# A new sequence of turns for a kernel of linear attention and an MLP, with the last chunk's buffers claimed by whoever comes first

## The chip, the core and the metric

The kernel runs on one core of one Trainium2 chip. A core has five engines that each work through their own instructions in order and wait for one another by semaphores: TensorE (PE, with its weight loads shown apart as PEld), VectorE (DVE), ScalarE (ACT), GpSimd (POOL) and SyncE (SP, which here only issues DMAs). The metric is the time of one execution on the device in microseconds (us); less is better. A line such as L857 is line 857 of the kernel's file.

## What is computed

A gated linear attention over B=4 batches, H=8 heads, S=768 steps and D=48 elements a head, then a layer norm and a two-layer network with ReLU and a residual, all in fp32:

```python
for t in range(S):
    state = alpha[:, :, t, :, None] * state + np.einsum('bhd,bhe->bhde', k[:, :, t], v[:, :, t])
    y[:, :, t] = np.einsum('bhd,bhde->bhe', q[:, :, t], state)
x = y.transpose(0, 2, 1, 3).reshape(B, S, H * D)          # 4 x 768 x 384
xn = (x - mu) / np.sqrt(var + 1e-06) * g_ln
out = x + np.maximum(xn @ w_ch1, 0.0) @ w_ch2             # 384 -> 1536 -> 384
```

The weights come in as float64.

## The kernel before

*Chunks and turns.* The 768 steps are cut into six chunks of 128. Each pair of chunk and batch has one Python generator of attention work, 24 in all; in the order string they are the letters a to x (a to d are chunk 0's batches, e to h chunk 1's, and so on). Each generator yields after every small step. Other letters stand for the network and the weights. The string ORDER (L33 to L53) has 1508 letters; the loop at L938 calls `next` on the generator of each letter, one after the other, under a manual schedule. So the string fixes the order in which instructions are issued on every engine at once: each engine works through its instructions in the order in which the turns emitted them. Nothing reorders them later. Buffers are handed out by pools with fixed counts; one that is reused makes its next writer wait for its last reader. One such pool holds six banks of PSUM (tag "bank", L353, L384, L452, L680, L851 and others) that all kinds of products share.

*An attention turn by turn.* Load q, k, v and alpha (`load`, L123 to L168); logarithm (L312) and running sums by a small matmul; exponentials on ACT (L324, L325); k and q scaled on DVE (L327, L329, "qk"); one gate row to DRAM and back; transposes to kT and qT, in chunks 0 and 1 by PE (L355, copied out at L360 and L362), later by DVE and DMA; the scores (L397 or L405, with the running sums of a later generator between them at L407); a masked copy into "at" (L415, L420); the state's update (L432 on PE, L445 on DVE, L447 on POOL). Then the **y product** (L463 and L467): 32 small matmuls into two banks, one with kT's state and one with the scores. ACT copies the first bank out (L493; L483 and L484 in the last two chunks) and DVE adds the second to it. Layer norm and a transpose give xT (L530 and L532 by PE in chunks 0 to 3). POOL zeroes "at" again at L499 for the last two batches of chunk 0.

*Weights.* Twelve pieces A to L are loaded as 64-bit words and turned into fp32 with integer operations on DVE (L219 to L236) and one on ACT (L227).

*The network.* For chunk 0 it is done directly: Y and Z are the two halves of the hidden layer (L567, three matmuls of 256 columns each), P and Q the second layer (L579 with an add at L583). For chunks 1 to 5 it runs by a bilinear algorithm that spends additions on fewer products. Turns "1" and "2" are the two row halves of the first layer: 15 **hidden products** for each chunk (`hidden_product`, L857, two matmuls of 256 columns), whose sums go to the hidden buffers with copies on ACT and adds on DVE and POOL (L864 to L900) and ReLUs on ACT (turns R and U, L907). Turn "M" is the second layer: 20 **products** for each chunk (`product`, L683), each four matmuls of 192 columns in one turn and in the next turn their adds into the output (L693 for an addition on DVE, L696 for a subtraction, L730 and others copies on ACT, L699 late adds on POOL, and a send to DRAM, L558). Operands of the products are sums of blocks: turn W combines the second weights (L643), S the first (L809), X the inputs of a chunk's hidden products (`combine_x`, L834, eleven turns a chunk), N the hidden blocks (`combine_hidden`, L670, sixteen turns a chunk, into buffers called sum0 to sum5 and in place). Turn O loads a kept x for the residual (L554).

*The last chunk's buffers.* Chunk 5's hidden buffers are not taken from the pools: `buffers_of_last` (L601) puts them together out of attention buffers that are no longer used (at, qk, eq), one more xT and three input buffers, once, at its first call; its callers are `third_of` (L595) and `combine_x` (L818). A hidden product of the last chunk takes its u buffers from `late_of["u"]` before it comes to `third_of`, so it needs the claim to have been made: in this order, the first last-chunk X turn is turn 1279, ahead of the first hidden product of that chunk.

Of the kernel before, what the change touches and what calls it, by code (L numbers as in the profile page):

```python
# [30 lines left out]


ORDER = (  # L33
    "bacabcadaacbcaadbcadabcababbebaccbadbaaBbccaedcbceAeeaaacbfecfBcdafddeaedbdeafae"
    "bcdccbfgadhAdcgCcdbebeebfhggdfgbfffbCdcgfgecdfchgdfhgabcddchdhAiiegjhacehedhhjfg"
    "biAdfidAeBhBijffYYiCjZZYYifZYlZCgjYDlYYjjZZYBZYgDieEgDgDjZZekEhZYGZgZigZGeeYgYgg"
    "fZYEhfGfkChihiYFYijfgEhgkhFZYhgYfghijgkFeZZlGZShfZYHlhHfYFYZeZHelYiZgllPmZkJIgJk"
    "PeiYjJIflHeSZIQgkIlYSjiPkffennSQlOKjLSnSjmSQhKnSjLnKPkiljnhSQnLkkjkWknkShOmPhkhl"
    "kOOhWlmmphmQmkmXjWQnXjlSQjPmkilXSXkP2OXWjXQjkjW2iXoSWX2oWX22Pi2mnol1j1mom2omSpoo"
    "l1XSpk2oW2m112p1m2pm11m1W211pp12O122r22jnn21lpnmnjSml1riOn2l12Rl111kqS1m21W1Rkp2"  # L40
    "o21mUXpq1mU2rUrnmj1rl2Rno2oomqonrormpokO1rNM2Mipin1op1ionoqUM2qp2W12RkMmNqiMoRtk"
    "UrpkqNM1NoMliMlNUMMNMNMKNqMlNorMWrnmtltNRMsqppMWNMriMMMpNlsqqqnoqttNttMtMsXMMssM"
    "sMNMNMX1oXXppMvstM2MXMMNMsppXoMXoqMsMMXM1nqqv11Xq1trMq2tqX21rn12v1r2ur2r222rvsqs"
    "svsu1rs1nuvvt2s11ss11p22rtsvosn2uropuXru222221uts212stnU1211u1121222Op1Rp2tRU21R"
    "Us1pXqU11x2tO2MM1vwMUM12xuRvu1vurNNNNwtOuuMwRxvNtxRNutwwMM2MOwNXwMNuXMMtNM1rMMMw"
    "qtXMMMxNUNxtMMsNMMMxXxMtXtrMMqMNrMXNvutMMwNuMMMNMMMxMLMOM11vvuq2X2O2wMus1wX11222"
    "2r2Xt1222w22utsqxvw2x2ww1vx21sX12121xwvq2O2x2w111u1uvU121w12s1wuRvx12U11J1q21R1U"
    "OvRxU121wMMu2xxsRNMw2NNMRM1MUNN2MMuUMqXN1MrNNRMNvMXNXMMMM2MMMxNM1uNXMMNMNMOXMXMv"
    "MMXOMMMXxNxwxMMvNMMMMMXMx21w1x222212v12w222x122w2212X11UX2212121121121wx111MU11X"
    "2RR2v1211212211R1URU211XOUM2XNRX1MX1RM2MXN2MXNXNMXXMXMMMN111U1MN1M1122MNM1MM2MM1"  # L50
    "11NNN121O11NM1MM21N1112N1122M1MMM12MM12N222M22M2RM1M2N22MM2MU1ON2M22M2UURR22RNNM"
    "MNM1MMOMRMNMUUM2ONMNNNMO2MMMUMNMMMMMRMMNNMMMNMNMMNMMMMMMMMNMNMMMMMMM"
)  # L53


# [1 line left out]
def kernel(  # L57
# [42 lines left out]
    NCB = S // P  # L100
# [491 lines left out]
    def third_of(c, t, h):  # L592

        if c + 1 == NCB:
            buffers_of_last()  # L595
            return late_of["h"][t * 2 + h]
        if c not in hT_of:
            hT_of[c] = work.tile([P, NJ, B, P], FP32, name="hT", tag="hT", bufs=1)
        return hT_of[c][:, t * NT:(t + 1) * NT, h * HB:(h + 1) * HB]

    def buffers_of_last():  # L601
        if "h" in late_of:
            return
        more_x = work.tile([P, NF, B, P], FP32, name="xT", tag="xT").rearrange("p f b t -> p (f b t)")
        free = [raw.tile([P, 2, 2, NP, D], FP32, name=f"r{n}", tag="in", bufs=7).rearrange(
            "t b i p d -> t (b i p d)") for n in "akq"]
        h = [t.rearrange("k p i s t -> k (p i s t)") for t in ats]
        h += [t.rearrange("t n p i c -> t (n p i c)") for t in qks[:3]]
        h.append(more_x[:, :NT * HB * P])
        late_of["h"] = [t.rearrange("p (j b t) -> p j b t", b=HB, t=P) for t in h]  # L610
        sums = [t.rearrange("t p i c -> t (p i c)") for t in eqs[:2]]
        sums += [more_x[:, NT * HB * P:]] + [t[:, 512:] for t in free]
        late_of["x"] = [t[:, i * HB * P:(i + 1) * HB * P]
                        for t in sums for i in range(t.shape[1] // (HB * P))]
        late_of["u"] = [t[:, :512] for t in free]
# [154 lines left out]
    def first_weights_ready():  # L770
        if "a" not in first_of:
            first_of["a"] = {n: [w1[:, 2 * t:2 * t + 2, f]]
                             for n, t, f in ((7, 2, 1), (10, 1, 0), (13, 0, 1), (8, 0, 0))}
        return first_of["a"]
# [5 lines left out]
    def x_ready(c):  # L780
        if ("b", c) not in first_of:
            b = x_blocks(c)
            first_of["b", c] = {0: b[3], 4: b[2], 6: b[0], 11: b[5], 12: b[1]}
        return first_of["b", c]
# [56 lines left out]

    def hidden_product(c, r, n):

        if n == FIRST[0]:
            for i in range(3):
                u = late_of["u"][i] if c + 1 == NCB else work.tile(
                    [P, 512], FP32, name="u", tag="sum", bufs=11)
                first_of["u", c, r, i] = u.rearrange("p (j t) -> p j t", j=2)
        cs = [third_of(c, t, h)[:, 2 * r:2 * r + 2].rearrange("p j b t -> p j (b t)")
              for t in range(3) for h in range(2)]  # L850
        acc = ps.tile([P, 2, HB * P], FP32, name="hps", tag="bank", bufs=6)  # L851
        a, b = first_weights_ready()[n], x_ready(c)[n]
        for i in range(2):
            j = 2 * r + i
            w = a[j // 2][:, 0] if len(a) == 2 else a[0][:, j // 2]
            w = w[:, j % 2 * P:][:, :P]
            nc.tensor.matmul(acc[:, i], w, b, start=True, stop=True)  # L857
        yield
        u0, u1, u2 = (first_of["u", c, r, i] for i in range(3))
        c0, c1, c2, c3, c4, c5 = cs  # L860
        add, sub = nc.vector.tensor_add, nc.vector.tensor_sub
        add_late, sub_late = nc.gpsimd.tensor_add, nc.gpsimd.tensor_sub

        if n == 3:  # L864
            nc.scalar.copy(out=c5, in_=acc)
        elif n == 7:
            add(c4, acc, c5)
        elif n == 5:
            add(c2, acc, c4)
        elif n == 1:  # L870
            add(u0, acc, c2)
        elif n == 10:
            nc.scalar.copy(out=u1, in_=acc)
        elif n == 9:
            sub(u2, u1, acc)
            add_late(c4, c4, u2)
        elif n == 4:
            sub(c2, c2, acc)
            add_late(c2, c2, u1)  # L879
        elif n == 14:  # L880
            add(u2, acc, u2)
            add_late(c0, u0, u2)
            add_late(c0, c0, c1)
        elif n == 6:
            add(c4, acc, c4)
        elif n == 11:
            nc.scalar.copy(out=c1, in_=acc)
        elif n == 2:
            add(c0, acc, c0)
        elif n == 13:  # L890
            sub(c3, u0, acc)
            add_late(c1, c1, c3)
        elif n == 8:
            sub(u2, u2, acc)
            add_late(c1, c1, u2)
            add_late(c5, c5, u2)
        elif n == 0:
            sub(c3, c3, acc)
        else:
            sub(c5, c5, acc)  # L900
        yield
# [8 lines left out]
    def hidden_products(r):  # L910
        for c in range(1, NCB):
            for n in FIRST:
                yield from hidden_product(c, r, n)
# [55 lines left out]
```

## Time and profile before

Three runs took 420.14, 420.69 and 421.5 us (median 420.69). The profiled execution took 420.64 us, of which 418.9 us is the span that the profile shows.

| what | us | share of the span | instructions |
|---|---|---|---|
| time of the profiled execution | 420.64 | | |
| its span | 418.9 | | 11553 |
| PE busy | 409.0 | 98% | 4608 |
| PE's weight loads busy | 360.9 | 86% | 4608 |
| DVE busy | 351.4 | 84% | 713 |
| ACT busy | 178.0 | 42% | 440 |
| POOL busy | 153.2 | 37% | 169 |

| line and work on PE | busy us | instructions |
|---|---|---|
| L857, hidden products with combined inputs | 46.3 of matmul | 192 |
| L857, hidden products with xT itself | 34.0 | 136 |
| L683, products (w, hT), (ws, sum), (ws, hT) | 40.5, 28.7, 23.6 | 224, 160, 128 |
| L579, second layer of chunk 0 | 33.0 | 96 |
| L567, first layer of chunk 0 | 32.5 | 144 |
| L463 and L467, y products | 22.0 and 22.7 | 320 each |

How to read it: the matmuls of PE overlap one another and their weight loads, so a line's busy sum is longer than the time that it adds to the span. A PE that is busy 98% of the time is in effect one long queue of matmuls; what a step costs there is read from the start of one instruction to the start of the next. The clock that was granted to TensorE is 1.00 in every stretch. HBM moves 140 GB/s as a mean over the span, most of it in the first half.

### The profile page before, as it was taken

The numbers are of one execution on the slowest core, as the hardware profiler recorded it, in microseconds if no ns is written. First come the engines' busy times: TensorE is split into PE (matmuls) and PEld (weight loads), VectorE is DVE, ScalarE is ACT, GpSimd is POOL, SyncE is SP. The second block draws the span as 40 slices with busy tenths as digits, with TensorE's granted clock in tenths as the row PEclk, the third lists the DMA queues.
The fourth block names the chain that finished last, engine by engine and source line by source line (L and its number), as shares of the span: only waits on it lengthen the run. The fifth ranks groups of instructions, "written<-read, shape, count | busy, mean of one in ns | idle before, by whom it ended". The sixth has DMA issues, their size and how long they took to land.

```text
span 418.9 us, 11553 instructions
## 1 busy us (share of the span) xinstructions
PE 409.0 (98%) x4608; PEld 360.9 (86%) x4608; DVE 351.4 (84%) x713; ACT 178.0 (42%) x440; POOL 153.2 (37%) x169
## 2 busy tenths in 40 slices
PE   6998999999999999999999999999999999999996
PEld 4787888766678889998889999889998899999996
DVE  3999999999999989996888996688876767977873
ACT  5498456724243496414546612364313242014110
POOL 3011000003203990043395033493152940499123
PEclk9999999999999999999999999999999999999999
DMA  7998889987778778587784546433035200001201
GB/s 247 325 297 246 206 201 293 287 194 181 145 221 176 200 167 185 128 195 178 146 215 70 130 105 166 88 95 77 0 114 104 67 1 2 0 20 38 94 20 56
DMA packets 133741, 59.52 MB, mean 142 GB/s; under 512 B 90764, under 2 KB 129804, under 8 KB 133688
## 3 DMA queue, kind: packets, MB, share of 16 engines
q1 hardware_dynamic: 133688, 58.79, 55.1%
q8 instruction: 36, 0.59, 0.6%
q14 instruction: 17, 0.14, 0.1%
HBM read 42.17 MB, written 16.61 MB: 140 GB/s over the span
## 4 chain that ended last, share of the span: by engine, by line
PE 89%; DVE 4%; ACT 2%; DMA 2%; issue 1%; SPq 1%; POOL 0%; POOLq 0%; DVEq 0%
PE hps L857 31%; PE ops L683 30%; PE ops L579 8%; PE hps L567 8%; PE aps L405 3%; PE yps L463 3%; PE yps L467 2%; PE sums L432 2%; DMA rq<-in_q_dram 2%; PE xps L530 1%; PE tps L355 1%; PE aps L397 1%; PE lps L407 1%; SPq L132 1%; DVE w L221 0%
## 5 line engine op out<-in xcount | busy, mean ns | idle before, releaser
L699 POOL TENSOR_TENSOR ob<-ob,u 128x192 f32<-128x192 f32 x40 | 26.3, 668 | 64.5 <-DVE ob L696 48.3
L857 PE MATMUL hps<-sum,w 128*128 128x256 f32 x192 | 46.3, 381 | 0.0
L907 ACT ACTIVATE hT<-hT 128x512 f32<-128x512 f32 x48 | 28.8, 624 | 34.9 <-POOL hT L879 18.5
L447 POOL TENSOR_TENSOR mid<-mid,gate 112x192 f32<-112x192 f32 x20 | 11.4, 568 | 80.0 <-DVE mid L445 33.3
L683 PE MATMUL ops<-w,hT 128*128 128x192 f32 x224 | 40.5, 327 | 0.0
L857 PEld LDWEIGHTS hps<-sum,w 128*128 128x128 f32 x192 | 36.1, 190 | 5.0
L683 PEld LDWEIGHTS ops<-w,hT 128*128 128x128 f32 x224 | 37.1, 190 | 0.7 <-issue 0.2
L857 PE MATMUL hps<-xT,w 128*128 128x256 f32 x136 | 34.0, 380 | 0.0
L579 PE MATMUL ops<-w,hT 128*128 128x384 f32 x96 | 33.0, 491 | 0.0
L567 PE MATMUL hps<-xT,w 128*128 128x256 f32 x144 | 32.5, 382 | 0.0
L567 PEld LDWEIGHTS hps<-xT,w 128*128 128x128 f32 x144 | 27.0, 190 | 4.2
L683 PE MATMUL ops<-ws,sum 128*128 128x192 f32 x160 | 28.7, 327 | 0.0
L857 PEld LDWEIGHTS hps<-xT,w 128*128 128x128 f32 x136 | 25.5, 190 | 3.1
L683 PEld LDWEIGHTS ops<-ws,sum 128*128 128x128 f32 x160 | 26.5, 190 | 0.3
L579 PEld LDWEIGHTS ops<-w,hT 128*128 128x128 f32 x96 | 17.6, 190 | 10.7 <-DVE w L236 0.3
L693 DVE TENSOR_TENSOR ob<-ops,ob 128x192 f32<-128x192 f32 x50 | 17.3, 353 | 10.6 <-PE ops L683 6.5
L447 POOL TENSOR_TENSOR st<-st,gate 112x192 f32<-112x192 f32 x16 | 11.7, 729 | 37.3 <-DVE st L445 25.9
L683 PE MATMUL ops<-ws,hT 128*128 128x192 f32 x128 | 23.6, 328 | 0.0
L463 PEld LDWEIGHTS yps<-st,qT 48*64 48x64 f32 x320 | 19.9, 134 | 4.0 <-issue 2.0
L467 PE MATMUL yps<-vx,at 64*64 64x48 f32 x320 | 22.7, 219 | 0.0
L463 PE MATMUL yps<-st,qT 48*64 48x48 f32 x320 | 22.0, 220 | 0.6 <-ACT x L493 0.6
L405 PEld LDWEIGHTS aps<-qT,kT 48*64 48x64 f32 x576 | 19.0, 134 | 4.1 <-issue 0.8
(255 smaller groups left out, 1134.2 us busy)
## 6 DMA issues: line engine op xcount, KB each, us to landing
ws<-in_moe_w_ch_dram SPq DMA_DIRECT2D x12, 768.0 KB, 5.9
td<-tr SPq DMA_DIRECT2D x64, 96.0 KB, 3.1
vn<-in_v_dram SPq DMA_DIRECT2D x12, 384.0 KB, 4.3
kept<-x SPq DMA_DIRECT2D x20, 192.0 KB, 3.0
ob<-kept SPq DMA_DIRECT2D x20, 192.0 KB, 3.1
out_dram<-ob SPq DMA_DIRECT2D x19, 192.0 KB, 1.9
ra<-in_alpha_dram SPq DMA_DIRECT2D x16, 192.0 KB, 2.6
kT<-td SPq DMA_DIRECT2D x32, 96.0 KB, 4.2
```

The costliest lines, as they stand in the source:

```text
L405: nc.tensor.matmul(to, kT[rs, p, s], qT[rs, p, s], start=True, stop=True)
L432: nc.tensor.matmul(up[h, p], qk_of(c, b)[ts, 1, p, i, :h.stop - h.start], vn[ts, i, p], start=True, stop=True)
L447: nc.gpsimd.tensor_mul(new, new, by)
L463: nc.tensor.matmul(yps[i][halves[s], i, p], qT[rs, p, s], (now, mid)[s][rs, p], start=True, stop=r != i)
L467: nc.tensor.matmul(yps[r][halves[s], i, p], at[halves[r], p, s], by, start=r != i, stop=True)
L567: nc.tensor.matmul(hps, w1[:, j // 2, f, j % 2 * P:][:, :P], xT_of[0][:, f, bs], start=(f == 0), stop=(f == NF - 1))
L579: nc.tensor.matmul(ops_of[b], hT_of[c][:, j, b], w2[:, j], start=(j == 0), stop=(j == NJ - 1))
L683: nc.tensor.matmul(acc, lhs[:, j], rhs[:, j], start=(j == 0), stop=(j == NT - 1))
L693: nc.vector.tensor_add(x, acc, x)
L699: getattr(nc.gpsimd, f"tensor_{op}")(x, x, y)
L857: nc.tensor.matmul(acc[:, i], w, b, start=True, stop=True)
L907: nc.scalar.activation(out=x, in_=x, func=AFT.Relu)
```

## The change

The change has two parts. Every letter occurs in the new ORDER as often as in the old one, so that each engine issues the same instructions, by line and by shape, with the same buffers and the same DMAs; only their sequence differs, nearly everywhere. And `hidden_product` calls `buffers_of_last` ahead of its u buffers if it belongs to the last chunk: in the new order turn 1303, a "2", is the first to touch that chunk's buffers, and its first X turn is 1306. In the new order lines behind L843 are two lines further down; line numbers in this text are those of before.

```diff
 ORDER = (
-    "bacabcadaacbcaadbcadabcababbebaccbadbaaBbccaedcbceAeeaaacbfecfBcdafddeaedbdeafae"
-    "bcdccbfgadhAdcgCcdbebeebfhggdfgbfffbCdcgfgecdfchgdfhgabcddchdhAiiegjhacehedhhjfg"
+    "aObcacabcaacaddbcaaaababbacdbbbacbccaeababdbcBcecedeaAeOfaacfbcebafcfddefBaeaddd"
+    "AeeccacbdccdbgdCcbbhgedeeccdhffagffgfcdfegCbagdddfghbdcfgbdahggbhiAeijbcehdehhhg"
...
-    "2RR2v1211212211R1URU211XOUM2XNRX1MX1RM2MXN2MXNXNMXXMXMMMN111U1MN1M1122MNM1MM2MM1"
-    "11NNN121O11NM1MM21N1112N1122M1MMM12MM12N222M22M2RM1M2N22MM2MU1ON2M22M2UURR22RNNM"
-    "MNM1MMOMRMNMUUM2ONMNNNMO2MMMUMNMMMMMRMMNNMMMNMNMMNMMMMMMMMNMNMMMMMMM"
+    "21v22RURx21u11221M22N1M2URXXMXXMXMXXR2NXUNM11RXNMN11MMM212212N11N12U1O11MMMMNXM1"
+    "MM1MMN11N12111M2NRX1NMM1M2M121111MNM2M22MM2212N22N22NM2O2M1M2MUMMU2ROMMM1UMRMJO2"
+    "NM2MM2RMN2N2RNMUUNMNO1MMNMNNMMMUMMRMMMMNNMMNMMMMNMMMNMMNMMMNMMMMMMMM"
 )
...
     def hidden_product(c, r, n):
 
+        if c + 1 == NCB:
+            buffers_of_last()
         if n == FIRST[0]:
             for i in range(3):
                 u = late_of["u"][i] if c + 1 == NCB else work.tile(
```

What moves where the prediction looks: three pairs of y products (chunk 2's batches 0, 2, 1 and then chunk 2's batch 3 with chunk 3's batch 0) become neighbours in PE's sequence; chunk 0's transposes, its L312 (ACT), L327 (DVE), L360 (DVE) and the first weight loads change places in the first 40 us; eight of the last chunk's X turns come ahead of the N turn that makes sum5 of chunk 4; and the first of the last two N turns comes ahead of the copy L741.

## The prediction

> **What bounds the kernel now.** I read the page's busy times first, then busy times in five stretches, then the chain of waits where PE pauses, then DVE's timeline at the end.
>
> The stretches (start:end in us, length, then busy us and count for PE, PE's weight loads, DVE, ACT, POOL, and the granted clock):
>
> ```profile
> 8.70:39.60 30.90, 28.43 (x552) 23.34 (x550) 29.57 (x57) 23.67 (x64) 3.09 (x4) 1.00 1.02 306
> 39.70:113.80 74.10, 74.10 (x902) 55.98 (x900) 72.47 (x129) 36.58 (x87) 10.54 (x13) 1.00 0.84 213
> 113.80:116.80 3.00, 2.38 (x130) 2.15 (x129) 3.00 (x7) 1.29 (x4) 0.00 (x0) 1.00 0.63 188
> 116.80:410.00 293.20, 293.10 (x2975) 269.71 (x2976) 240.98 (x502) 111.70 (x277) 133.35 (x136) 1.00 0.44 106
> 410.00:418.90 8.90, 5.68 (x35) 5.38 (x34) 2.99 (x7) 0.32 (x1) 2.87 (x5) 1.00 0.19 66
> ```
>
> The reader is to see that PE is idle for 2.5 us in the first of these stretches, 0.62 us in the short third one, 0.1 us in the 293 us behind it, and 3.2 us at the end. From 39.7 us the kernel is PE's instruction stream, end to end, at a clock of 1.00. DVE is second: 72.47 of 74.1 us up to 113.8, about 82% afterwards. So a new sequence can win only at the two ends and at that one pause, and can lose wherever it lets PE wait. The chain of waits shows the pause:
>
> ```profile
> 114.99 0.07 PE yps L467
> 115.08 0.50 ACT x L493
> 115.58 0.04 issue
> 115.62 0.25 PE yps L463
> ```
>
> Two y products (L463/L467, 32 matmul instructions each) stand next to each other in PE's sequence. The second may not start before ACT has copied the first out of PSUM (L493, 0.50 us). PE could have gone on at 114.85 and went on at 115.62: 0.77 us lost. This happens once.
>
> The chain before the stream of large products starts:
>
> ```profile
> 36.38 0.28 DVE st L445
> 36.70 0.52 PE sums L432 x26
> ...
> 39.28 0.47 PE aps L405 x17
> 39.75 2.36 PE hps L567 x10
> ```
>
> and DVE's timeline at the end (start, us, line, operation, what ended the idle time):
>
> ```profile
> 411.14 0.68 DVE L670 TENSOR_TENSOR sum<-sum,at 128x512 f32<-128x512 f32 x1
> 411.86 0.69 DVE L670 TENSOR_TENSOR sum<-sum,sum 128x512 f32<-128x512 f32 x1
> 412.47 0.35 DVE L693 TENSOR_TENSOR u<-ops,u 128x192 f32<-128x192 f32 x1
> ...
> 415.96 0.36 DVE L693 TENSOR_TENSOR ob<-ops,ob 128x192 f32<-128x192 f32 x1 [1.12 <-POOL ob L699]
> ```
>
> **The change, part by part.** All sums are against the profiled execution, 420.64 us (span 418.9 and 1.7 around it); the median of the runs shown, 420.69, is the same within 0.05. Instruction counts by line and shape are unchanged on all engines (PE 2360, DVE 685, ACT 411, POOL 165, SP 390 DMAs). So only places move.
>
> *The claim of the last chunk's buffers.* It issues nothing. In the new order a hidden product of the last chunk (turn 1303 of 1508) comes before that chunk's first X turn (1306), so it must claim. A claim can only make the first writer of a buffer wait for its last reader. Those are attention rows, and the last y product ends at 282 us in the old order and stands some 9 us later in PE's new stream, about 40 us ahead of that turn (332); this distance is the cover. Cost 0; without it, the first adds on DVE (L869, 0.69 us) would wait, and the next products behind them, by as much as the readers are late.
>
> *The first 39.7 us.* PE's 324 instructions ahead of the first L567 are the same in both orders. So are the 56 DVE instructions from the first L327 to the third L233 of the first weight piece; laid out at their usual start-to-start steps they take 28.9 us in either. Before, they ran from 8.75 to 39.59, 30.84 us; so 1.9 us of waits. I followed the new order row by row with the old durations. L360 of the first kT now stands ahead of L327 and waits 0.4 us for its transposes. The next such copy, 0.5 us late before, is on time. The zeroing of at (POOL L499, 0.95 us), during which an L219 took 1.18 us instead of 0.55, falls two DVE rows further on and costs about 0.4 instead of 0.6. SP has the second gate load moved ahead of the first weight load; that load is issued some 0.5 us later and is read a microsecond later, so it hides. I take -0.2 us. Bounds: -1.9 (all waits gone) and +1.0 (ACT's L227 for the first piece now stands behind one more L312, 0.5, and a row load that lands late, 0.5).
>
> *PE's changes between small and large matmuls.* Attention work that stands alone costs more than merged: a group of L432 alone between large products took 0.505 us, L405/407 alone 1.079, the two together 1.437, so a merge saves 0.147. Leaving out visits of transposes alone (0.327 each, the bare sum of three), PE makes 25 visits to small matmuls behind the first L567 in the old order and 24 in the new. -0.15 us (bounds -0.4 and +0.2, a few neighbours change).
>
> *Y products next to each other.* This is the largest term. The old program has one y product whose wait names the L493 of the y product directly ahead of it. The new one has three: chunk 2's batches 0, 2 and 1 now follow each other without a break (two waits), and chunk 2's batch 3 is directly followed by chunk 3's batch 0 (one). Where the old order had a block of L579 (2.78 us) or a group of L432 between two of them, now nothing stands. Each repeats the measured case: last matmul of the first product, ACT copy 0.50, restart, 0.77 us in which nothing else can run, since PE works in order. Three for one: +1.55. Bounds: 0, if the buffers come free in another order than the waits name; +2.8, if ACT is in a 0.62 us L907 or L513 each time.
>
> *The pause at 153.5* (0.26 us, an L857 pair behind a late L493) has no counterpart: -0.25, bounds -0.26 and 0.
>
> *Chunk 4's product 13.* In the old order its operand (L670, sum5) was ready at 303.93 and its matmul started at 308.24: 4.3 us in hand. In the new order eight L834 of the last chunk are pulled ahead of it on DVE, and it stands behind an L696 that waits for POOL. Counting from the add of the product that stands four ahead of the very last y product in PE's sequence: 38 DVE instructions, 15.0 us at their steps (ten L670 at 0.60, eight L834 at 0.335, twelve adds at 0.265, the rest 3.1), about 0.6 for pairs that depend on each other, and a POOL wait of about 1. PE has in the same stretch thirteen products at 1.30, a y product of 1.1 and a hidden product of 0.86, 18.9 us from the first matmul, 17.4 from that add. The 4.3 us are gone; whether PE waits hangs on tenths. I take +0.4, bounds 0 and +1.6. What stands behind: the four products of that chunk that follow and POOL's last adds on ob.
>
> The upper bound comes from these rows, POOL's timeline with L699 first beside L670s (two in 2.01) and then alone, and the slowest L670 (ns, min/median/max):
>
> ```profile
> 302.38 2.01 POOL L699 TENSOR_TENSOR ob<-ob,u 128x192 f32<-128x192 f32 x2 [15.70 <-DVE ob L696]
> 305.66 0.59 POOL L699 TENSOR_TENSOR u<-u 128x192 f32<-128x192 f32 x1 [1.28 <-DVE u L733]
> ```
>
> ```profile
> L670 DVE TENSOR_TENSOR sum<-qk x1: 1768/1768/1768, 387.9 to 387.9; 128x512 f32<-128x512 f32 x1
> ```
>
> Alone an L699 takes 0.59 us, beside L670s about 1.0; an L670 is 0.69 as a rule and was 1.77 once. In the new order the L696 ahead of sum5 releases a POOL L699 just as sum5 starts, so 0.6 to 1.1 us can come on top. The Trainium skill (SBUF — State Buffer, "SBUF: two separate sides") states this as an exclusive lock: a VectorE operation with two SBUF inputs and a GpSimd operation that reads SBUF hold a shared port pair for a whole instruction, and the other blocks. The stretched rows above agree with it; by that rule this term would be 1.0 to 1.5 and not 0.4, the sum 422.8.
>
> *Short loops.* At about 230 us two products (2.60 us) now stand where a chain of 2.84 must pass: start of a product to its sum 1.5, ACT copy L730 0.37, L693 0.27, L670 0.70; so 0.24 late. At 61, 120 and 280 us waits on ACT copies become as short as their chains. None is over 0.3 by its rows. +0.3 together, bounds 0 and +1.0.
>
> *The end.* The two L670 at 411.14 held the L693 at 412.47 up, and POOL's five L699 behind it made the last L693 wait until 415.96, where its matmul (start 414.22, 1.5 us to the add) allowed 415.72. In the new order the first of the two L670 stands ahead of L741, where DVE idled 0.88 us. -0.25, bounds -0.3 and 0.
>
> Sum: -0.2 - 0.15 + 1.55 - 0.25 + 0.4 + 0.3 - 0.25 = +1.4: **422.0 us**. All other hand-overs to PE that I worked out up to 180 us keep at least the room that they had before, so DVE, though 97% busy there, does not become the bound.
>
> **The rivals.**
>
> *No measurable change (0.3% is 1.26 us, about what a measurement of this kernel can tell):* the y waits are paid, but chunk 4 and the short loops cost nothing. 420.64 + 1.4 - 0.7 = 421.3. For it: DVE keeps idling 18% of the time after 116.8, and one pause of PE gives all later operands the same respite. Against: nothing gives those 0.77 us back to PE, whose stream has no other gap to absorb them.
>
> *Faster:* the start. If the DVE waits between 8.75 and 39.59 vanish, the first L567 starts at 37.8 and all that follows with it; with the y waits at half their price: -1.9 - 0.15 + 0.8 - 0.25 - 0.25 = -1.75, 418.9. It decides from a first L567 earlier than 38.2. For it: that stretch holds 1.9 us of waits that are not work. Against: most of them are waits for transposes and loads that the new order keeps at the same distance; the chain there also passes through PE's own L405 (39.28), and ACT is busy 23.67 of 30.9.
>
> *Much slower:* POOL and DVE hold each other up at chunk 4 (its upper end, +1.2 more), and ACT is busy at the y waits (+1.2 more): 424.4. For it: the stretched rows; against: ACT is under half busy from 100 to 140 us.
>
> *That the order does nothing,* since the slowest engine is the same: PE's sum of steps differs by 0.15, so this is the second case.
>
> **How the numbers follow.** Forecast 0.38, much slower 0.14, no measurable change 0.28, faster 0.20. The forecast's own range is 421.9 to 423.4, which with the much slower case makes 0.52 for slower by over 0.3%. Below lies 0.20, and between 0.28. For 8 in 10 the range takes in the forecast and the middle case whole (0.66) and at least half of each outer one: from just above the faster case's time to somewhat beyond the much slower one's, 419.0 to 425.0 (all lower bounds together give 417.8, all upper ones 427.2).
>
> **What would show it.** L493 as what ends PE's wait at L463/L467: three times 0.77 us near 112 to 116 and 136, with PE's busy time in those windows short by as much. The first L567 between 39.2 and 40.0. A PE gap ahead of one L683 group near 306, ended by DVE L670. The last L693 released by PE and not by POOL. I am wrong if PE shows one L493 wait or none, if the first L567 moves by over 1 us, or if a wait of PE on a load or on DVE ahead of 180 us appears.

## The result, and the profile after

The changed kernel takes 423.66 us (median of 6 runs, 422.69 to 424.3) against 420.71 for the kernel before (6 runs, 419.64 to 421.8): a ratio of 1.0068 with a 95% interval from 1.0046 to 1.009, some 2.9 us more. Its profiled execution took 423.38 us, span 421.7; the one before took 420.64, span 418.9. Lines behind L843 of the kernel before are two further down in the changed one (L857 is L859). This text keeps a profile's own numbers in its lines and uses the numbers of before in its sentences.

The changed kernel's stretches, with the same columns as before (start:end, length, then busy us and count for PE, PE's weight loads, DVE, ACT, POOL, the granted clock, DMA share and GB/s):

```profile
8.70:40.50 31.80, 28.33 (x543) 23.69 (x543) 30.56 (x58) 23.80 (x64) 2.51 (x3) 0.95 0.99 300
40.60:113.90 73.30, 73.30 (x871) 55.42 (x870) 70.88 (x124) 35.59 (x85) 8.08 (x13) 1.00 0.89 213
113.90:117.40 3.50, 2.37 (x142) 2.12 (x135) 3.50 (x8) 0.98 (x2) 0.14 (x1) 1.00 0.75 202
117.40:139.00 21.60, 21.60 (x324) 17.62 (x319) 20.11 (x40) 10.02 (x24) 5.35 (x7) 1.00 0.73 183
139.00:141.00 2.00, 1.45 (x83) 1.27 (x74) 1.55 (x5) 1.48 (x4) 2.00 (x2) 1.00 0.91 135
141.00:412.70 271.70, 271.51 (x2640) 251.51 (x2638) 217.53 (x463) 102.43 (x253) 126.67 (x130) 1.00 0.40 99
412.70:421.70 9.00, 5.90 (x37) 5.61 (x35) 2.38 (x6) 0.32 (x1) 3.11 (x6) 1.00 0.18 66
```

PE again works without a break from the first L567 on, except in the third and the fifth stretch, where it loses 1.13 and 0.55 us. What ends these waits is one line of the view of PE's waits between 40.9 and 415 us, which has no other entry (total, times, longest):

```profile
PE yps L467 <- ACT x L493: 1.7, 3, 0.6
```

The new thing is in the first stretch: its mean granted clock is 0.95, not 1.00. Cut finer (same columns):

```profile
29.22:32.63 3.41, 3.14 (x82) 2.73 (x72) 3.34 (x6) 3.35 (x13) 0.88 (x1) 1.00 1.03 312
32.63:36.05 3.42, 1.19 (x9) 1.01 (x10) 3.42 (x9) 2.60 (x8) 0.47 (x1) 1.00 0.98 237
36.05:39.46 3.41, 3.41 (x48) 2.62 (x50) 3.38 (x8) 2.37 (x5) 0.04 (x1) 0.50 0.91 287
39.46:42.87 3.41, 3.41 (x78) 3.11 (x78) 3.37 (x8) 1.96 (x4) 0.00 (x0) 1.00 0.54 80
```

In the second of these stretches PE is busy 1.19 of 3.42 us: it had finished the head's early work and waited twice, for L519 and for L329 on DVE. For the next 3.41 us its clock is half, and it then has work all the time. The same work, from the transposes L355 to the first L567, in the kernel before, in the changed one and in the changed one with transposes repeated in the gap (an experiment below):

```profile
35.24:39.69 4.45, 4.30 (x118) 3.69 (x116) 4.42 (x11) 3.70 (x9) 1.19 (x2) 1.00 0.96 256
```

```profile
35.38:40.82 5.44, 5.44 (x115) 4.58 (x115) 5.41 (x12) 3.75 (x6) 0.51 (x1) 0.69 0.78 220
```

```profile
35.10:39.13 4.03, 3.99 (x116) 3.54 (x116) 4.00 (x10) 3.12 (x6) 0.51 (x1) 1.00 0.95 275
```

At full clock the new order does this work in 4.0 us, at a mean of 0.69 in 5.4. So the halved clock costs 1.4 us in this execution, and the first L567 comes at 40.82 in place of 39.69, although DVE finished the first weight piece 0.4 us earlier than before (third L233 done at 39.26 against 39.68).

From the two profiles: +1.13 up to the first L567; +1.79 from there to the start of the last matmul (377.46 against 375.67, of which 1.5 are the y waits); -0.18 behind it. The sum is 2.74, by which the spans differ (2.8 between their rounded figures).

### The profile page after: what moved, and what is told of

The parts are those of the page before. It is cut to its first block, busy times and chain, and to the rows that moved or that the text cites. A ratio compares the mean times of both kernels' runs of the same rounds, so it can differ in the third digit from the quotient of the medians.

```text
span 421.7 us, 11565 instructions
## 1 busy us (share of the span) xinstructions
PE 411.4 (98%) x4608; PEld 362.3 (86%) x4608; DVE 349.7 (83%) x713; ACT 179.7 (43%) x440; POOL 151.2 (36%) x169
## 4 chain that ended last, share of the span: by engine, by line
PE 89%; DVE 4%; DMA 1%; issue 1%; ACT 0%; POOL 0%; SPq 0%; DVEq 0%; POOLq 0%
PE hps L859 31%; PE ops L683 28%; PE hps L567 8%; PE ops L579 7%; PE aps L405 3%; PE yps L463 3%; PE yps L467 2%; PE sums L432 2%; PE xps L530 1%; PE lps L407 1%; PE tps L355 1%; PE yps L458 1%; DMA rq<-in_q_dram 1%; PE aps L397 1%; DMA td<-tr 0%
## 5 line engine op out<-in xcount | busy, mean ns | idle before, releaser
L699 POOL TENSOR_TENSOR ob<-ob,u 128x192 f32<-128x192 f32 x40 | 27.2, 690 | 59.1 <-DVE ob L696 45.6
L859 PE MATMUL hps<-sum,w 128*128 128x256 f32 x192 | 46.5, 381 | 0.0
L909 ACT ACTIVATE hT<-hT 128x512 f32<-128x512 f32 x48 | 28.5, 624 | 39.7 <-POOL hT L881 12.9
L447 POOL TENSOR_TENSOR mid<-mid,gate 112x192 f32<-112x192 f32 x20 | 12.5, 625 | 86.8 <-DVE mid L445 49.5
L683 PE MATMUL ops<-w,hT 128*128 128x192 f32 x224 | 40.3, 327 | 0.1
L859 PEld LDWEIGHTS hps<-sum,w 128*128 128x128 f32 x192 | 36.0, 190 | 5.0
L683 PEld LDWEIGHTS ops<-w,hT 128*128 128x128 f32 x224 | 37.2, 190 | 1.2 <-DVE hT L670 0.4
L859 PE MATMUL hps<-xT,w 128*128 128x256 f32 x136 | 33.7, 380 | 0.0
L567 PE MATMUL hps<-xT,w 128*128 128x256 f32 x144 | 32.5, 382 | 0.0
L693 DVE TENSOR_TENSOR ob<-ops,ob 128x192 f32<-128x192 f32 x50 | 17.5, 351 | 16.7 <-PE ops L683 8.8
L567 PEld LDWEIGHTS hps<-xT,w 128*128 128x128 f32 x144 | 27.0, 190 | 3.9
L683 PE MATMUL ops<-ws,sum 128*128 128x192 f32 x160 | 28.8, 327 | 0.0
L859 PEld LDWEIGHTS hps<-xT,w 128*128 128x128 f32 x136 | 25.3, 190 | 2.9
L683 PEld LDWEIGHTS ops<-ws,sum 128*128 128x128 f32 x160 | 26.4, 190 | 0.2
L447 POOL TENSOR_TENSOR st<-st,gate 112x192 f32<-112x192 f32 x16 | 9.5, 593 | 42.2 <-DVE st L445 42.2
L683 PE MATMUL ops<-ws,hT 128*128 128x192 f32 x128 | 23.7, 328 | 0.0
L405 PE MATMUL aps<-qT,kT 48*64 48x64 f32 x576 | 22.9, 227 | 0.0
L467 PE MATMUL yps<-vn,at 64*64 64x48 f32 x320 | 22.6, 220 | 0.0
```

What stands on the lines that cost most here:

```text
L405: nc.tensor.matmul(to, kT[rs, p, s], qT[rs, p, s], start=True, stop=True)
L447: nc.gpsimd.tensor_mul(new, new, by)
L467: nc.tensor.matmul(yps[r][halves[s], i, p], at[halves[r], p, s], by, start=r != i, stop=True)
L567: nc.tensor.matmul(hps, w1[:, j // 2, f, j % 2 * P:][:, :P], xT_of[0][:, f, bs], start=(f == 0), stop=(f == NF - 1))
L683: nc.tensor.matmul(acc, lhs[:, j], rhs[:, j], start=(j == 0), stop=(j == NT - 1))
L693: nc.vector.tensor_add(x, acc, x)
```

## The experiments

Each kernel ran with the kernel before on the same chip, in three groups, each on another chip, whose medians for the kernel before were 420.64, 421.22 and 420.75. An execution is called *dipped* here when its mean clock was 0.997 or less: one stretch of 3.41 us at half clock in 421.7 makes 0.996.

| kernel | median us | ratio to before, 95% | dipped | median at full clock |
|---|---|---|---|---|
| before, all groups | 420.84 | | 22 of 95 | 420.49 |
| changed, both times | 423.61 | 1.0055 (1.0036 to 1.0075) | 11 of 18 | 422.69 |
| changed, y products apart | 421.96 | 1.0021 (0.9996 to 1.0045) | 5 of 12 | 421.48 |
| changed, transposes repeated | 423.60 | 1.0069 (1.0045 to 1.0092) | 1 of 8 | 423.58 |
| before, y products apart | 421.64 | 1.0014 (0.9985 to 1.0043) | 6 of 12 | 419.82 |
| new head, rest of before | 421.10 | 1.0007 (0.9989 to 1.0025) | 4 of 12 | 420.61 |
| old head, rest of changed | 422.24 | 1.0026 (1.0008 to 1.0044) | 2 of 12 | 422.21 |
| old head, y products apart | 420.82 | 0.9994 (0.9975 to 1.0013) | 2 of 12 | 420.56 |
| before, apart and filled | 420.70 | 0.9999 (0.9979 to 1.0018) | 0 of 12 | 420.70 |
| changed, filled | 423.67 | 1.0066 (1.0040 to 1.0091) | 0 of 6 | 423.68 |
| changed, apart and filled | 422.04 | 1.0025 (1.0010 to 1.0041) | 0 of 12 | 422.04 |
| before, longer idle | 420.56 | 1.0001 (0.9972 to 1.0029) | 1 of 12 | 420.09 |
| before, apart, filled, end moved | 420.58 | 0.9993 (0.9978 to 1.0009) | 2 of 12 | 420.38 |

**The changed kernel again.** No edit.

> The changed kernel once more, for a second profile and more times. Its first profile shows PE idle from 32.4 to 34.0 and from 34.5 to 35.4 us, then a granted clock of 0.50 from 36.05 to 39.46, and the first L567 at 40.82 (39.69 before). Theory A (the new head lets PE idle so long that the clock is halved, about 1.3 us): most executions show a mean clock of about 0.996, and a profile with the dip has its first L567 near 40.8, one without it near 39.5. Theory B (the late start comes from DVE and loads, and the dip is an accident that hides in idle time): the first L567 is near 40.8 with and without the dip. Three waits of L463/L467 on L493, 0.8 us each, in either.

11 of 18 executions dipped in all, two of them twice. Within this kernel, executions at full clock have a median of 422.69 (7), with one dip 423.69 (9), with two 425.15 (2); within the kernel before, 420.49 (73) and 422.11 (22). So a dip goes with 1.0 to 1.6 us between medians. It is not all that varies: the seven executions of the changed kernel at full clock lie between 422.15 and 424.30. The second profile shows two dips in a row (same columns):

```profile
31.33:34.74 3.41, 1.45 (x12) 1.00 (x10) 3.38 (x7) 3.38 (x10) 0.00 (x0) 1.00 1.05 288
34.74:38.16 3.42, 2.84 (x30) 2.52 (x32) 3.38 (x8) 1.63 (x4) 0.51 (x1) 0.50 0.91 250
38.16:41.57 3.41, 3.41 (x79) 2.96 (x75) 2.89 (x6) 2.69 (x4) 0.00 (x0) 0.50 0.42 103
```

The first L567 was at 42.08 there, and not at 40.8: the halved clock is there, as theory A said, but the theory did not have that it can stay down for a second stretch. Both profiles of this kernel have a dip; what its head does without one is seen in the exchanged heads below. The y waits are the same three.

**The y products apart.**

```diff
-"...QPWoQiXWnkimPXoXjWlkj1SQiX..."
+"...QWoQiXWnPkimPXoXQjWlkj1SiX..."
...
-"...2nlrlSpUjm..."
+"...nl2rlSpUjm..."
```

> The changed kernel, with only three of PE's steps moved: two blocks of L579 (turns P7 and Q7) now stand between the three y products near 113 to 117 us, and one hidden product (turn 2, its 17th) between those near 139. Theory A (each pair of neighbours costs 0.8 us because PE can do nothing else during the copy): all three waits go, 1.6 to 2.4 us less than the changed kernel, about 421.4. Rival (PE loses the same time elsewhere, since what follows is late by DVE or ACT): waits vanish but the time stays within 0.5 us of the changed kernel.

1.65 less than the changed kernel in the medians of that group, as theory A said. The waits are gone; the places where they were (same columns):

```profile
115.00:119.00 4.00, 4.00 (x74) 2.56 (x73) 3.94 (x8) 0.64 (x2) 0.00 (x0) 1.00 0.69 139
119.00:142.00 23.00, 23.00 (x400) 18.53 (x398) 21.82 (x43) 11.07 (x27) 6.57 (x8) 1.00 0.83 197
```

PE is busy through both. From the first L567 to the start of the last matmul this execution took 375.88 us, 1.58 less than the changed kernel's 377.46 and 0.2 more than the kernel before; no wait came in elsewhere. The three waits were 2.3 us, so 0.7 of it did not come back. Where the pairs stood, the two profiles differ by 0.99 for the two near 115 us and by 0.51 for the one near 140: a pair costs some 0.5 us net. What takes the other part when the y products stand alone between large matmuls was not measured.

**The y pair of before apart.**

```diff
-"...mkilXSXkP..."
+"...mkPilXSXk..."
```

> The kernel before, with its own one pair of neighbouring y products separated by a block of L579 (turn P7 moved between them). Theory A: the 0.8 us wait at 115 us goes, 419.9 against 420.7. Rival: the wait moves to the next user of the bank and the time stays at 420.7.

Inconclusive as a time: 421.64, with 6 of 12 executions dipped, though its head is that of before. At full clock the median is 419.82 against 420.49, and in the profile no wait of PE on L493 is left between 39 and 415 us. The wait did not move on to another place. But from the first L567 to the last matmul this profile has 375.34 us against 375.67, only 0.33 less, so here too a part of the wait's 0.8 did not come back. The gain at full clock, 0.7, is smaller than what the dips do.

**Transposes repeated in the gap.**

```diff
-            for f in range(NF):
+            for f in [*range(NF)] * (3 if (c, b) == (0, 1) else 1):
                 nc.tensor.transpose(xps[:, f], xn[:, f * P:(f + 1) * P], ident)
```

> The changed kernel, with the three transposes L530 of chunk 0's batch 1 repeated twice more into the same bank, which fills PE's idle time from 34.5 to about 35.4 us and alters no value. Theory A (the clock is halved because PE idles too much of one stretch): mean clock 1.00 in all executions, first L567 near 39.5, time about 1 us below the changed kernel although there is more work. Rival (the clock has another cause, or the start is bound by DVE): no gain, or 0.1 to 0.3 us more.

Both theories miss a part. The clock stayed up (7 of 8 executions), and the first L567 came at 39.13, as theory A said. The time did not fall. PE's waits behind the first L567 in the profiled execution (424.51 us, 0.9 above this kernel's median) show what came instead:

```profile
PE yps L467 <- ACT x L493: 1.7, 3, 0.6
PE hps L567 <- issue: 0.8, 1, 0.8
PE hps L859 <- issue: 0.6, 1, 0.6
PE aps L405 <- issue: 0.5, 1, 0.5
```

Three new pauses, 1.9 us together, at 59.4, 70.2 and 197.4 us, which the profile puts down to nothing ("issue"). All stand in or just behind a run of attention's small matmuls.

The kernel has six more transposes on PE, so the places at which PE's instructions are loaded fall elsewhere in its work. The traces show this loading as packets of 16 KB in a queue of the kind "instruction", 36 in each execution, about one for every 256 of PE's records (matmuls, weight loads and semaphore instructions). Matmul by matmul, this execution falls behind the changed kernel's profile at four places: at the three pauses and at 231.7 us, by 0.69, 0.96, 0.76 and 0.33 us. That is 2.74 of the 2.82 us that it takes longer from the first L567 to the last matmul (380.28 against 377.46). Counted from the start, the four places are records 1729, 2240, 5569 and 6592 of PE: whole multiples of 256 apart, give or take one. With the packets counted in order, one to a place, the packet for each of the four had landed only 1.4 to 1.6 us before PE went on; at all other such places of this execution it had landed at least 2.1 us before. So these pauses go with instructions that arrive late, and not with the work around them. That packet and place belong together is inferred from the counts. The added instructions are not needed for it: the kernel with y products apart, without any, has a pause of 0.41 us put to "issue" at 31.22, at record 704, where the packet had landed 1.4 us before. Why the packets come closer in some executions is open.

**Heads exchanged.** The order up to the first Y of one kernel, then the turns of the other that are left, in their sequence: the new head on the old rest, the old head on the new rest, and the latter with the y products apart. No line of code differs from the changed kernel.

> The new order's turns up to its first Y (168 of 1508), then all turns of the order before that are left, in their own sequence. Theory A (the new head itself costs time, because PE idles 2.4 us of a stretch of 3.4 near 32 to 35 us and its clock is then halved): about half of the executions with a mean clock of 0.996 or less, against about one in six for the kernel before, and a median 0.8 to 1.5 us above it, near 421.8. Rival (all of the loss lies behind the first L567): the median of the kernel before, 420.7, within 0.4.

> The order before up to its first Y (176 turns), then all turns of the new order that are left. Theory A: the three y waits stay (1.6 us more than before) and the head's loss goes, so about 422.2, 1.4 less than the changed kernel. Rival (an earlier first L567 only makes PE wait later, on DVE's weights up to 113 us): waits of PE on L233, L236 or loads appear between 40 and 113 us and the time stays near 423.4.

> As the one above, with the three pairs of y products separated too. Theory A (head and y products are all of the difference, and they add up): 420.6, within 0.5 of the kernel before. Rival (something else in the new middle or end costs): over 421.3.

The last two came out as theory A had them: 422.24 (422.2 expected) and 420.82 (420.6 expected). Their difference, 1.42, is what separating the y products gives, a second time. With the old head and the y products apart, nothing is left of the loss. The first fell to the rival: 421.10 against 421.22, with 4 of 12 dipped. Its profile has two idle times in the head (1.67 and 0.87 us) like the changed kernel's (1.55 and 0.88), but the clock stayed at 1.00 and the first L567 came at 39.54. The stretches of 3.41 us, counted from the point at which the clock first shows as 1.00 there:

```profile
30.35:33.76 3.41, 2.14 (x41) 1.65 (x29) 3.34 (x7) 3.18 (x11) 0.00 (x0) 1.00 1.04 341
33.76:37.17 3.41, 2.13 (x35) 1.78 (x37) 3.41 (x9) 2.88 (x6) 0.51 (x1) 1.00 0.67 120
```

A boundary fell between the two idle times, so each stretch was 0.63 busy. In the changed kernel both fell into one, 0.35 busy. The changes of the clock lie a whole number of 3.413 us apart in every profile, from a start that differs between executions (4.0 to 7.2 us). The Trainium skill (TensorE: Matmul & The Clock Gate, "Part 1: The HAM clock gate (the "warmup" mystery)") says that the window is 3413 ns long and free-running, and does not start with the kernel; the traces agree with both.

How busy a stretch has to be is not quite settled. On this grid of 3.41 us, in all 14 profiles, five stretches at full clock in the first 50 us were followed by half the clock. PE was busy 0.35 of the time in the changed kernel (at 32.63), 0.43 in its second profile (31.33), 0.36 and 0.42 in the one with y products apart (7.41 and 34.72), and 0.50 in the old head with y products apart:

```profile
33.20:36.60 3.40, 1.71 (x16) 1.32 (x15) 3.40 (x9) 3.33 (x11) 0.51 (x1) 1.00 1.02 232
36.60:40.10 3.50, 3.49 (x71) 3.05 (x75) 3.46 (x8) 1.78 (x5) 0.84 (x2) 0.51 0.81 247
```

Four stretches of like share were not: 0.42 (at 4.76 us) and 0.45 (32.07) in the kernel that follows, 0.45 in the last of the filled kernels (4.55) and 0.47 in the old head with y products apart (5.92). Three of these four are the first stretch of the grid. At full clock none of 0.52 or more was followed by half, and at the end of the span all of 0.26 or less were. So between 0.42 and 0.50 PE's busy share alone does not decide.

**The idle time of before made longer.**

```diff
-"...dfhgabcddcdhAii..."
+"...dfhgacddcbdhAii..."
```

> The kernel before with one turn moved: the transposes of chunk 0's batch 1 (turn b, its 23rd) come after those of batch 2 instead of ahead, so that PE idles from 32.9 to 34.9 us, 0.35 us longer, and has three more transposes behind the gap. Theory: PE's busy share of a 3.4 us stretch falls from 0.50 at least to about 0.4, and the share of executions with a mean clock of 0.996 or less rises from about a quarter to a half; median up by 0.4 for the transposes and 0.4 for the clock, near 421.7. Rival (dips have nothing to do with this gap): a quarter as before, 421.1.

A miss: 420.56 against 420.75, and 1 of 12 dipped. The gap is longer, 1.88 us, and the stretch with it less busy, but the clock stayed:

```profile
32.07:35.48 3.41, 1.53 (x15) 1.50 (x14) 3.41 (x9) 3.35 (x10) 0.51 (x1) 1.00 1.10 261
35.48:38.90 3.42, 3.42 (x110) 2.97 (x109) 3.38 (x8) 2.68 (x6) 0.67 (x1) 1.00 0.92 292
```

One gap of 1.9 us was not enough in 11 of 12 executions; the new head's two gaps (1.55 and 0.88 in the changed kernel's profile) went with a dip in about half of theirs. The three transposes moved behind the gap did not show in the time either.

**The gap filled with three matmuls of constants.** In the kernel before with its y products apart, in the changed kernel, in the changed kernel with y products apart, and in the first of these with the N turn of the end moved as the new order has it. The edit for the new order is shown; with the order of before the batch is 2 instead of 1.

```diff
+            for _ in range(3 if (c, b) == (0, 1) else 0):
+                nc.tensor.matmul(xps[:, :2], ident, consts[:, :2 * P], start=True, stop=True)
             for f in range(NF):
                 nc.tensor.transpose(xps[:, f], xn[:, f * P:(f + 1) * P], ident)
```

> The kernel before with its pair of y products separated, and with three matmuls of constants (256 columns) issued ahead of the transposes of chunk 0's batch 2, into the bank that those then overwrite; they fill PE's idle time from 33.3 to 34.6 us. Theory A: the executions with a halved clock become fewer (about half of that kernel's 12 executions without the fill had a mean clock of 0.995 or 0.996), those that remain come from idle time before 10 us; median near 420.0, below the kernel before. Rival: the extra PE instructions cost as much, as in the kernel with repeated transposes, whose undisturbed times were 0.9 above the changed kernel's; 420.8 or more.

> The changed kernel with three matmuls of constants (256 columns) ahead of the transposes L530 of chunk 0's batch 1, into the bank that those overwrite: PE then works through most of its first idle time near 32 to 34 us. Theory (the clock is halved after a stretch of 3.4 us in which PE was busy less than about half): hardly any of 12 executions with a mean clock of 0.996 or less, against 11 of 18 for the changed kernel; the three y waits stay; median about 422.5, some 1 us below the changed kernel. Rival (the halved clock lies in time that PE would lose anyway, and added PE instructions cost as in the kernel with repeated transposes): 423.4 or more.

> The same fill, and the three pairs of y products separated: 12 executions nearly all at a full clock, median about 420.9, no different from the kernel before. Rival: the new order has a further loss behind the first L567, then 421.5 or more.

> The kernel before with its y pair separated, the fill of the gap near 33 to 35 us, and the last but one N turn ahead of the M turn with L741, as the new order has it: 0.8 less for the y wait, 0.2 less at the end, and no halved clock, about 419.9 against 420.9. Rival: the fill costs what the y wait gives, 420.8.

The dips went nearly as expected: 0 of 12, 0 of 6, 0 of 12 and 2 of 12. With the repeated transposes that is 1 of 26 where the new head's gap is filled, against 20 of 42 with the new head as it is (changed, y products apart, new head on old rest). With the old head it is 2 of 24 filled, against 22 of 95 in the kernel before. The times did not follow. With the new order the rivals won: 423.67 is the changed kernel's time, and 422.04 that with the y products apart. With the old order 420.70 and 420.58 lie between theory (420.0 and 419.9) and rival (420.8). In the filled changed kernel, PE's waits behind the first L567 (a line behind L530 is two further down, so L685 is L683 of before) are

```profile
PE yps L467 <- ACT x L493: 1.7, 3, 0.6
PE ops L685 <- DVE qk L327: 0.6, 1, 0.6
PE sums L432 <- DVE st L445: 0.6, 1, 0.6
```

One is a real one, on DVE's L445 at 107.5 us. The other, at 231.4, names an L327 that ended 0.4 us before PE went on. The filled kernel with y products apart has it too (0.39 at 228.1), and so have the two filled kernels with the old order (0.19 at 227 and 228): in all four it stands at record 6592 or 6593 of PE, where the kernel with repeated transposes is held up too. It is a pause of the kind described there, though a packet that landed 1.2 to 1.4 us before its place also occurs in these kernels with next to no pause. The profiled execution of the filled changed kernel (424.67, 1.0 above its median) also starts late: its first L567 comes at 40.02 although the clock stays at 1.00, because a L432 ahead of the fill waits 1.18 us until 31.94 and PE then works without a break through the fill (1.55 us) to L567. With the y products apart and the gap filled it comes at 39.15.

So a filled gap keeps the clock, and what is won ahead of L567 is spent again. The 1.63 between the medians of the two filled kernels with the new order is what separating the y products gives, for the third time. None of these kernels beats the kernel before: the best ratio is 0.9993 (0.9978 to 1.0009).

## Why the prediction came out as it did

The direction, slower, and the range, 419.0 to 425.0, held; the size was half: 422.0 was forecast, 423.66 measured. By the steps of the prediction:

*Y products next to each other, +1.55.* Right in mechanism, and in the size of the wait. Three waits on L493 with about 0.77 us lost each, less 0.8 for the old one, is 1.5 in the profiles. What a pair costs in all is less. The kernels with the y products apart have no such wait, not even the old one, so 2.3 us should have gone; 1.65, 1.42 and 1.63 went in three pairs of kernels (1.2, 1.65 and 1.64 at full clock), some 0.5 for each pair.

*The first 39.7 us, -0.2, bounds -1.9 and +1.0.* This is the step that failed. The profile has +1.13, outside these bounds, and a first L567 that moves by over 1 us is one of the signs that the prediction itself gave for being wrong. What the order does to the instructions was sized about right: 39.49 had been worked out for the first L567, and where the clock stayed up the new head had it at 39.54 (on the old rest) and at 39.13, 39.15 and 40.02 with the gap filled. Missing was that PE's idle time has a price of its own. The new order finishes the early attention work sooner and idles longer near 33 us (1.55 and 0.88 us against 1.57). The prediction followed the new order with the old durations, and so took a clock of 1.00 for granted. The idle time halved the clock of the work that follows: 1.4 us in the profiled execution. Over many executions 11 of 18 of the changed kernel dipped and 22 of 95 of the kernel before. So the median of the one is a dipped execution (423.69 with one dip) and that of the other is not (420.49). Of the 2.8 us between the medians of all executions (423.61 against 420.84), 0.6 vanish if only executions at full clock are compared (422.69 against 420.49, 2.2). That is still 0.8 more than the forecast's 1.4. With seven executions that spread over 2 us, it is not shown whether this rest is real, nor what it is.

*Changes between small and large matmuls, -0.15.* It cannot be told. What is left of the +1.79 us behind the first L567, once the y waits, the pause and the short loops are taken out, is about -0.1, and the two profiles of the changed kernel differ there by 0.2 (377.46 and 377.66).

*The pause at 153.5, -0.25.* A shorter one came in its place (0.15 at 154.9), so -0.11.

*Chunk 4's product 13, +0.4.* The mechanism was there, the wait was not. DVE's timeline at sum5, and POOL's (start, us, line):

```profile
308.95 0.35 DVE L696 TENSOR_TENSOR u<-u,ops 128x192 f32<-128x192 f32 x1 [0.79 <-POOL u L699]
309.22 0.69 DVE L670 TENSOR_TENSOR sum<-hT,sum 128x512 f32<-128x512 f32 x1
309.82 1.09 DVE L670 TENSOR_TENSOR sum<-sum,hT 128x512 f32<-128x512 f32 x1
```

```profile
309.38 1.98 POOL L699 TENSOR_TENSOR ob<-ob,u 128x192 f32<-128x192 f32 x2 [0.47 <-DVE u L696]
```

L696 waits 0.79 us for POOL, as the prediction had it. The L670 of sum5 is the one at 309.22: it took its usual 0.69 us although POOL's L699 stood beside it from 309.38, and the L670 behind it, which is not sum5's, took 1.09. So the operand was there at 309.91, and the product started at 310.30: 0.4 us to spare, of 4.3. "Hangs on tenths" was right, and it fell on the cheap side. The prediction's own count had 0.8 to spare (16.6 us on DVE and POOL against 17.4 on PE), and its +0.4 went against that count. The dear case, in which sum5 itself is stretched, did not come.

*Short loops, +0.3.* One of 0.26 at 235.9 (worked out as 0.24 at 230) and one of about 0.25 at 194.5 that was not on the list. At 61, 120 and 280 us, which were on it, no wait of PE shows. With +0.5 the sum is within the bounds.

Together these four middle terms were forecast at +0.3, and the profiles have 1.79 - 1.5 = +0.3. That is luck in part: chunk 4's +0.4 did not come, and the pause and the loops made up for it.

*The end, -0.25.* 0.18 less behind the last matmul's start. The first of the two L670 ran in DVE's idle time and the last L693 waited for PE, as said:

```profile
411.25 0.68 DVE L670 TENSOR_TENSOR sum<-sum,at 128x512 f32<-128x512 f32 x1
412.14 0.36 DVE L741 TENSOR_TENSOR u<-ops,u 128x192 f32<-128x192 f32 x1 [0.21 <-PE ops L683]
...
418.71 0.36 DVE L693 TENSOR_TENSOR ob<-ops,ob 128x192 f32<-128x192 f32 x1 [0.94 <-PE ops L683]
```

The same move in the kernel before (the last row of the table) took the part behind the last matmul's start from 3.56 to 3.41 us in the profiles; its median cannot be told from that of the kernel before.

*The claim, 0.* No wait of over 0.2 us shows near turn 1303 or anywhere behind 240 us.

Of the rivals, "faster" named its own test, a first L567 earlier than 38.2; it came at 40.82. "No measurable change" was right that chunk 4 costs nothing, and "much slower" came nearest in time (424.4) for reasons that have no part in it.

What stays open: new head and new rest together, with y products apart, are 1.3 above the kernel before of the same group (421.96 and, filled, 422.04), while each half joined to a half of the other order is not (421.10 against 421.22, and 420.82). For the unfilled one the interval of the ratio includes 1, and 5 of its 12 executions dipped; at full clock 421.48 stands against 420.39 for the kernel before of that group. In its profile nothing is lost behind the first L567: from there to the end of the span it takes 379.28 us, against 379.25 in the kernel before. For the filled one no execution dipped; its profile has some 1.0 us more behind the first L567 than the unfilled one (376.85 against 375.88), 0.46 of it at record 6593. The profiled execution is 0.9 below the median, so what holds up the others is not shown.

## What to carry to other kernels

Idle time of the bounding engine ahead of its long stream is not free on PE: look at how it is spread over any 3.4 us, because two gaps that fall into one stretch can halve the clock of the work behind them, and whether they fall into one differs from one execution to the next. Work put into such a gap keeps the clock, but look behind it: here pauses at places where PE's instructions are loaded took much of the gain. Compare executions with their clocks beside them: medians of two kernels can differ because one dips in most of its runs and the other in few. And when two users of a bank become neighbours on an engine that works in order, count the whole copy between them, each time (0.77 us here for a copy of 0.50), and what separating them costs in turn (some 0.25 here).

## What had not been expected of the hardware

- Half of TensorE's clock for 3.41 us, after a stretch of 3.41 us in which PE was busy 0.35 to 0.50 of the time and never idle for longer than 1.67 us at once (2.17 in the case near 9 us). After 0.52 and more at full clock it never came; from 0.42 to 0.47 it stayed away four times. Two low stretches in a row occurred after 0.43 and then, at half clock, 0.83.
- Six more matmuls on PE, placed where it idles, went with pauses of 0.1 to 0.8 us far from there, next to runs of small matmuls and with no work that they wait for. They stand whole multiples of 256 of PE's records apart, where a packet of 16 KB in the queue for instructions had landed 1.3 to 1.6 us before PE went on.
